# Wo and the broadcast reciprocal denominators loaded in whole-column pieces of 128 partitions, with one write of the reciprocals

## The chip, the cores and the metric

The kernel runs on one core of a Trainium2 chip. The metric is device time in microseconds (us). The core has a matrix engine (PE), a vector engine (DVE), an activation engine (ACT), GpSimd (POOL) and a sequencer without arithmetic (SP) that issues almost all DMAs of this kernel. One DMA is carried out by up to 16 DMA engines that the core has. On-chip memory is SBUF, 128 partitions of which each holds a row of every tile; matrix products land in PSUM, eight banks of 128 x 512 fp32.

## The reference

One transformer block over x of 2048 tokens by 1024, in bf16: an adaptive layer norm, linear attention with 32 heads of 32, a second adaptive layer norm, and a gated feed-forward part of width 3584.

```python
mod = (silu(c) @ w_mod).reshape(1, 6, 1, -1)
sa, ca, ga, sb, cb, gb = mod[:, 0], ..., mod[:, 5]

h = layernorm(x) * (1 + ca) + sa
q, k, v = heads(h @ wqkv)                    # 32 heads of 32
pq, pk = phi(q), phi(k)                      # phi(t) = (t + 1 if t > 0 else exp(t)) + 1e-6
kv = einsum('bhsd,bhse->bhde', pk, v)        # per head a 32 x 32 matrix
z  = einsum('bhsd->bhd', pk)
num = einsum('bhqd,bhde->bhqe', pq, kv)
den = einsum('bhqd,bhd->bhq', pq, z)[..., None] + 1e-6
x = x + ga * ((num / den).reshape(1, 2048, 1024) @ wo)

h = layernorm(x) * (1 + cb) + sb
x = x + gb * ((silu(h @ w_gate) * (h @ w_up)) @ w_down)
```

## The kernel before

**How it is written.** Operations are added in one program order to a small planner (`_Prog`, from line 120). Each engine carries out its own operations in that order. The planner derives from the SBUF intervals and PSUM banks that an operation touches which earlier operations of other engines it must wait for; partitions are not told apart. A DMA has a lane (a semaphore). An operation with `ninc=4` issues four DMAs on one lane, and a reader waits until all four have landed. Nearly all instructions are emitted through one helper, so in the profile they carry its line, 176, and are told apart by tile names.

**The stages.** From about 12 to 126 us: first layer norm, the q and k products, phi. From 126 to 186 us: sixteen groups `g_group(0..15)`, each of 16 matmuls, form G, the product of the normalized x and phi(k), for two halves of the heads (g 0 to 7 and g 8 to 15). From 186 to 220 us: the output projection `wo_part` with its residual. The rest, to 826 us: the feed-forward part in four chunks of 512 tokens.

**What lies in the stage of the change.** The loop `for g in range(16)` (from line 1038) sets the order on all engines:

- After group 0, `z_row` (line 962) writes the z row to DRAM and reads it back broadcast (`zb<-z_row`), and `wo_load(0)`, `wo_load(1)` (line 934) load Wo, 1 MB each, into the tile `wo` [128, 8, 1024]. Partition 32g+e and column block 4f+h of it hold row 512f + 128g + 32h + e of Wo.
- After group 1, `den()` (line 970) forms the denominators in PSUM bank 7 (partition 32ch + head, 512 tokens of chunk ch), adds 1e-6, takes the reciprocal and a bf16 copy `rcb`, writes it to the DRAM tensor `recip_den` [32, 2048], lets SP wait for that write, and loads it back broadcast over 32 partitions a head into `rb` [128, 8, 2048], 4 MB in eight DMAs. Both the write and the loads are issued on SP.
- At g 6 to 9, DVE scales Wo by ga, two column blocks each (`fold_ga`, line 1020).
- At g 7 to 14, DVE multiplies phi(q) by the reciprocals, one of eight head groups each (`scale_pq(g-7)`, line 992; in the profile `pqt<-pqt,rb`).
- DVE also empties the bank of each group (`g_evac`, line 953; `g<-ps,modcol,gtmp`), from g 6 on that of the group just before, and it does so ahead of that step's `fold_ga` and `scale_pq`.
- At g 10, `kvt_mm(0)` (line 995) needs G of groups 0 to 7; at g 11 and 12, `m_mm(0, ..)` (line 1005) multiplies its result by half of Wo into `mw`.
- At g 10, SP issues `stgx1`, 2 MB of w_mod into space that `rb` held, once `scale_pq(3)` is through.
- After group 15: SP reloads x into `xres`, in pieces; PE goes on with six matmuls of `wo_part`, then `kvt_mm(1)`, which needs G of groups 8 to 15, so `g_evac(15)`.

The DRAM view of Wo that the loads take is this (line 390), and `RDR` is `recip_den`:

```python
wov = A_wo.rearrange("(f g h e) n -> f g e h n", f=2, g=4, h=4)
```

Of the kernel before, what the change touches and what calls it, by code (L numbers as in the profile page):

```python
# [262 lines left out]
def bass_adaLN_cond__linear_attn_block__swiglu_ffn__prompt_kernel(  # L263
# [12 lines left out]
    S, D = A_x.shape[1], A_x.shape[2]  # L276
# [3 lines left out]
    NCH = 4  # L280
    NDT = D // 128
    NFT = F // 128
    NHG = D // 128
    EPS = 1e-5

    with ExitStack() as es:
# [6 lines left out]
        def T(name, off, shape, dt):  # L293
            n = 1
            for s_ in shape[1:]:
                n *= s_
            assert off % 32 == 0 and off + n * mybir.dt.size(dt) <= ARENA, (name, off, shape)
            return nc.alloc_sbuf_tensor_at(name, shape, dt, offset=base + off)
# [38 lines left out]
        RB = T("rb", 72 * KB, [128, NHG, S], BF16)  # L337
        WV = T("wv", 104 * KB, [128, NDT, D], BF16)
        HT = T("ht", 120 * KB, [128, 2, NDT, 512], BF16)
        WO = T("wo", 120 * KB, [128, NHG, D], BF16)  # L340
# [22 lines left out]
        RCB = T("rcb", 204 * KB, [128, 512], BF16)  # L363
# [18 lines left out]
        RDR = nc.dram_tensor("recip_den", [32, S], BF16).ap()  # L382
# [7 lines left out]
        wov = A_wo.rearrange("(f g h e) n -> f g e h n", f=2, g=4, h=4)  # L390
# [6 lines left out]
        P = _Prog()  # L397
# [534 lines left out]
        phi_flush()  # L932

        def wo_load(f):
            outs = [WO[32 * g:32 * g + 32, 4 * f:4 * f + 4, :] for g in range(4)]

            def fn(e, outs=outs, f=f):
                return [e.dma_start(out=o_, in_=wov[f, g]) for g, o_ in enumerate(outs)]

            P.add("sp", fn, reads=[], writes=outs, lane="wo%d" % f, ninc=4, tag="wo")  # L940

        G_BANKS = [0] + [next_bank() for _ in range(4)]

# [26 lines left out]
        def den():  # L970
            for hg in range(NHG):
                for ch in range(NCH):
                    P.pe("matmul", out=PS[32 * ch:32 * ch + 32, 7, :], lhsT=ZSEL[:, hg * 32:hg * 32 + 32],
                         rhs=PQT[:, hg, ch * 512:(ch + 1) * 512], start=(hg == 0), stop=(hg == NHG - 1),
                         skip_group_check=True)
            P.dve("tensor_scalar", out=DEN[:], in0=PS[:, 7, :], scalar1=1e-6, scalar2=None, op0=ALU.add)
            P.dve("reciprocal", out=RCP[:], in_=DEN[:])
            P.dve("tensor_copy", out=RCB[:], in_=RCP[:])
            wr = [P.dma("rdr%d" % ch, RDR[:, ch * 512:(ch + 1) * 512], RCB[32 * ch:32 * ch + 32, :])
                  for ch in range(NCH)]  # L980
            P.wait_for("sp", wr)
            for gh in range(2):
                outs = [RB[32 * hh:32 * hh + 32, 4 * gh:4 * gh + 4, :] for hh in range(4)]
                ins = [RDR.rearrange("(g x) s -> x g s", x=4)[hh, 4 * gh:4 * gh + 4].unsqueeze(0).to_broadcast([32, 4, S])
                       for hh in range(4)]

                def fn(e, outs=outs, ins=ins):
                    return [e.dma_start(out=o_, in_=i_) for o_, i_ in zip(outs, ins)]

                P.add("sp", fn, reads=[], writes=outs, lane="rb%d" % gh, ninc=4, tag="rb")  # L990

        def scale_pq(hg):
            P.dve("tensor_tensor", out=PQT[:, hg, :], in0=PQT[:, hg, :], in1=RB[:, hg, :], op=ALU.mult)
# [44 lines left out]
        for g in range(16):  # L1038
            g_group(g)
            while ev < g + 1 - (3 if g < 4 else 2 if g < 6 else 1):  # L1040
                g_evac(ev)
                ev += 1
            if g == 0:
                z_row()
                for f in range(2):
                    wo_load(f)
            if g == 1:
                mod_red()
                mod_fin_col(2, True)
                den()  # L1050
            if 6 <= g <= 9:
                fold_ga(2 * (g - 6))
                fold_ga(2 * (g - 6) + 1)
            if g == 10:
                kvt_mm(0)
            if 11 <= g < 13:
                m_mm(0, g - 11, [MB, 7, G_BANKS[4], 6])
            if 7 <= g < 15:
                scale_pq(g - 7)
            if g == 10:  # L1060
                P.dma("stgx1", STGX[0][:], wmv[:, :, 3072:4096])
# [51 lines left out]
        for st in range(NST):  # L1113
# [3 lines left out]
            if st < 4:  # L1117
                P.wait_for("sp", [done])
                if st < 3:
                    ch = st + 1  # L1120
# [127 lines left out]
```

## Time and profile before

| | us |
|---|---|
| median of 3 runs (lowest, highest) | 828.01 (827.72, 828.80) |
| the profiled execution | 827.71 |
| its span in the profile | 826.0 |
| PE busy | 816.3 |
| DVE busy | 312.2 |
| ACT busy | 197.0 |
| POOL busy | 41.0 |
| share of the time of 16 DMA engines taken by SP's queue | 53.8% |

Times inside the profile count from the start of the span; the execution's own time is 1.7 us more than the span. PE is busy for 99% of the span, and its granted clock is 1.00 in the stretch from 120 to 210 us. A matmul of 128 x 512 starts about 0.216 us after the one before it; the 379 ns that the profile gives for one include the time it takes to drain. "Landing" is the time from the issue of a DMA to its completion at its semaphore. "DMA share" is the mean busy share of the 16 DMA engines in a stretch of time; it can come out a little over 1.

### The profile page before, as it was taken

How to read it: one execution, taken by the hardware profiler on the slowest of the kernel's cores; microseconds unless marked ns; L12 is line 12 of the kernel's file. 1: busy time of each engine (PE TensorE's matmuls, PEld its weight loads, DVE VectorE, ACT ScalarE, POOL GpSimd, SP SyncE). 2: the span in 40 equal slices, each digit the busy share in tenths (PEclk: the TensorE clock that was granted, in tenths of full speed). 3: DMA queues.
4: the chain of work that ended last, by engine and by line, in shares of the span. 5: the costliest groups of instructions: out<-in, count | busy, mean ns of one | idle time of the engine just before them, and what ended most of it. 6: DMA issues, size and time to landing. Idle time of an engine off the chain costs nothing.

```text
span 826.0 us, 10436 instructions
## 1 busy us (share of the span) xinstructions
PE 816.3 (99%) x4243; PEld 375.9 (46%) x4322; DVE 312.2 (38%) x672; ACT 197.0 (24%) x338; POOL 41.0 (5%) x58
## 2 busy tenths in 40 slices
PE   8999999999999999999999999999999999999998
PEld 4544444444444444444444444444444444444444
DVE  5798988477945521111221112122111111221111
ACT  4758642123341111011111101111110111111011
POOL 1110000000130000020000003000000300000000
DMA  9969756865698995600455570045557004553000
GB/s 316 297 139 223 167 159 149 181 175 211 149 253 245 296 249 153 166 26 26 136 151 151 153 174 25 23 131 153 151 152 182 27 19 126 151 152 88 0 26 26
DMA packets 199392, 119.32 MB, mean 144 GB/s; under 512 B 58024, under 2 KB 183088, under 8 KB 199344
## 3 DMA queue, kind: packets, MB, share of 16 engines
q1 hardware_dynamic: 199328, 118.65, 53.8%
q8 instruction: 34, 0.56, 0.3%
q14 instruction: 14, 0.11, 0.0%
q10 hardware_dynamic: 16, 0.00, 0.0%
HBM read 100.67 MB, written 4.33 MB: 127 GB/s over the span
## 4 chain that ended last, share of the span: by engine, by line
PE 98%; issue 1%; DMA 0%; DVE 0%; POOL 0%; SPq 0%
PE ps L176 98%; DMA xres<-in_A_x_dram 0%; POOL rstd L176 0%; DVE xres L176 0%; DVE stats L176 0%; SPq L176 0%; DVE ht L176 0%; DVE ve L176 0%; DVE mv L176 0%; DVE modcol L176 0%
## 5 line engine op out<-in xcount | busy, mean ns | idle before, releaser
L176 PE MATMUL ps<-h2t,gug 128*128 128x512 bf16 x878 | 210.1, 379 | 0.9
L176 PE MATMUL ps<-h2t,guu 128*128 128x512 bf16 x878 | 209.9, 379 | 0.9
L176 DVE TENSOR_TENSOR at<-sg,ps 128x512 bf16<-128x512 bf16 x112 | 77.0, 687 | 282.8 <-PE ps L176 270.6
L176 ACT ACTIVATE sg<-ps 128x512 bf16<-128x512 f32 x112 | 66.9, 597 | 309.7 <-PE ps L176 298.3
L176 PEld LDWEIGHTS ps<-h2t,guu 128*128 128x128 bf16 x896 | 87.7, 98 | 105.7
L176 PEld LDWEIGHTS ps<-h2t,gug 128*128 128x128 bf16 x896 | 87.6, 98 | 105.5
L176 PE MATMUL ps<-wd_a,at 128*128 128x512 bf16 (+1 forms) x502 | 111.9, 377 | 0.5
L176 PE MATMUL ps<-ht,wqk 128*128 128x512 bf16 x499 | 110.7, 379 | 0.9 <-DVE ht L176 0.2
L176 PE MATMUL ps<-wd_b,at 128*128 128x512 bf16 (+1 forms) x377 | 84.6, 377 | 0.4
L176 PEld LDWEIGHTS ps<-wd_a,at 128*128 128x128 bf16 x512 | 50.1, 98 | 59.6
L176 DVE TENSOR_TENSOR ut<-att,gb_b 128x512 bf16<-128x512 bf16 (+1 forms) x32 | 13.6, 426 | 167.5 <-ACT att L176 167.5
L176 PEld LDWEIGHTS ps<-ht,wqk 128*128 128x128 bf16 x512 | 49.2, 98 | 58.9 <-DVE ht L176 1.0
L176 ACT ACTIVATE att<-ps 128x512 bf16<-128x512 f32 (+1 forms) x32 | 17.4, 591 | 182.1 <-PE ps L176 182.1
L176 PEld LDWEIGHTS ps<-wd_b,at 128*128 128x128 bf16 x384 | 37.6, 98 | 44.7
L176 PE MATMUL ps<-pk,xres 128*128 128x512 bf16 x250 | 55.4, 379 | 0.6 <-issue 0.5
L176 PE MATMUL ps<-mw,pqt 128*128 128x512 bf16 x249 | 55.4, 379 | 0.5 <-issue 0.2
L176 POOL TENSOR_SCALAR h2t<-h2t,modcol 128x512 bf16<-128x512 bf16 x32 | 26.5, 846 | 383.0 <-DMA h2t<-xn 383.0
L176 ACT ACTIVATE e<-ps 128x512 bf16<-128x512 f32 x56 | 33.3, 611 | 31.8 <-PE ps L176 15.8
L176 ACT ACTIVATE junk<-xres 128x1024 bf16<-128x1024 bf16 x26 | 27.6, 1063 | 45.9 <-DVE xres L176 34.2
L176 PEld LDWEIGHTS ps<-mw,pqt 128*128 128x128 bf16 x256 | 24.8, 98 | 30.0 <-issue 0.5
L176 PEld LDWEIGHTS ps<-pk,xres 128*128 128x128 bf16 x256 | 24.6, 98 | 30.1 <-issue 1.3
L176 DVE SCALAR_TENSOR_TENSOR xres<-ps,xres 128x512 bf16<-128x512 f32 x32 | 21.5, 688 | 11.6 <-PE ps L176 11.3
(111 smaller groups left out, 337.8 us busy)
## 6 DMA issues: line engine op xcount, KB each, us to landing
gug<-in_B_w_gate_dram SPq DMA_DIRECT2D x56, 512.0 KB, 4.0
guu<-in_B_w_up_dram SPq DMA_DIRECT2D x56, 512.0 KB, 5.3
xres<-in_A_x_dram SPq DMA_DIRECT2D x20, 256.0 KB, 4.4
rb<-recip_den SPq DMA_DIRECT2D x8, 512.0 KB, 11.7
stgx<-in_w_mod_dram SPq DMA_DIRECT2D x2, 2048.0 KB, 9.3
wd_a<-in_B_w_down_dram SPq DMA_DIRECT2D x4, 1024.0 KB, 7.7
out_dram<-xres SPq DMA_DIRECT2D x31, 128.0 KB, 1.7
xres<-in_A_x_dram SPq DMA_DIRECT2D x3, 1024.0 KB, 6.5
```

Source lines behind the costliest of these rows:

```text
L176: return getattr(e, method)(**kw)
```

## The change

All three transfers keep their bytes and their contents; their cut is another.

- Wo: four DMAs per half as before, but each brings one column block of all 128 partitions (128 rows of 2 KB), where before it brought four column blocks of 32 partitions (32 x 4 rows of 2 KB). On the DRAM side a piece is now a pattern of 4 x 32 rows: g steps by 128 rows, e by one.
- The reciprocals are written by one DMA from 128 partitions, where four wrote 32 partitions each. On the DRAM side the pattern is 4 chunks x 32 heads x 512 elements.
- The broadcast: eight DMAs as before, each now one head group hg for all 128 partitions: four rows of `recip_den`, each repeated 32 times (a step of 0). Before, each brought four head groups for 32 partitions. Each DMA has a lane of its own, so `scale_pq(hg)` waits for one DMA, where it waited for the four of its half.

```diff
         def wo_load(f):
-            outs = [WO[32 * g:32 * g + 32, 4 * f:4 * f + 4, :] for g in range(4)]
+            outs = [WO[:, 4 * f + h, :] for h in range(4)]
 
             def fn(e, outs=outs, f=f):
-                return [e.dma_start(out=o_, in_=wov[f, g]) for g, o_ in enumerate(outs)]
+                return [e.dma_start(out=o_, in_=wov[f, :, :, h, :]) for h, o_ in enumerate(outs)]
 
-            P.add("sp", fn, reads=[], writes=outs, lane="wo%d" % f, ninc=4, tag="wo")
+            P.add("sp", fn, reads=[], writes=[WO[:, 4 * f:4 * f + 4, :]], lane="wo%d" % f, ninc=4, tag="wo")
...
-            wr = [P.dma("rdr%d" % ch, RDR[:, ch * 512:(ch + 1) * 512], RCB[32 * ch:32 * ch + 32, :])
-                  for ch in range(NCH)]
-            P.wait_for("sp", wr)
-            for gh in range(2):
-                outs = [RB[32 * hh:32 * hh + 32, 4 * gh:4 * gh + 4, :] for hh in range(4)]
-                ins = [RDR.rearrange("(g x) s -> x g s", x=4)[hh, 4 * gh:4 * gh + 4].unsqueeze(0).to_broadcast([32, 4, S])
-                       for hh in range(4)]
+            wr = P.dma("rdr", RDR.rearrange("h (c s) -> c h s", c=NCH), RCB[:])
+            P.wait_for("sp", [wr])
+            for hg in range(NHG):
+                rb_ = RB[:, hg, :]
+                rows = RDR[4 * hg:4 * hg + 4, :].unsqueeze(1).to_broadcast([4, 32, S])
 
-                def fn(e, outs=outs, ins=ins):
-                    return [e.dma_start(out=o_, in_=i_) for o_, i_ in zip(outs, ins)]
+                def fn(e, rb_=rb_, rows=rows):
+                    return [e.dma_start(out=rb_, in_=rows)]
 
-                P.add("sp", fn, reads=[], writes=outs, lane="rb%d" % gh, ninc=4, tag="rb")
+                P.add("sp", fn, reads=[], writes=[RB[:, hg, :]], lane="rb%d" % hg, tag="rb")
```

## The prediction

> **What bounds the kernel now.** First the chain of work that ended last, on the page:
>
> ```profile
> PE 98%; issue 1%; DMA 0%; DVE 0%; POOL 0%; SPq 0%
> ```
>
> PE is the bound, so a transfer counts only where PE waits for it. I then asked for PE's waits from 125 to 205 us, the stretch that holds all changed transfers, and for DVE's:
>
> ```profile
> PE ps L176 <- issue: 0.6, 4, 0.2
> DVE pqt L176 <- DMA rb<-recip_den: 6.6, 1, 6.6
> ```
>
> The reader sees that PE loses 0.6 us there in four gaps, none to a DMA. DVE does wait 6.6 us for `rb`, but PE doesn't feel it. Thus nothing in this change can win more than 0.6 us; the question is what it can lose. The order of time of DVE, PE and SP shows how much room there is:
>
> ```profile
> 149.30 4.02 SPq L988 DMA_DIRECT2D rb<-recip_den  x8
> 161.28 1.22 DVE L176 TENSOR_TENSOR pqt<-pqt,rb 128x2048 bf16<-128x2048 bf16 x1 [6.65 <-DMA rb<-recip_den]
> 180.49 1.21 DVE L176 TENSOR_TENSOR pqt<-pqt,rb 128x2048 bf16<-128x2048 bf16 x1
> 186.07 0.75 DVE L176 SCALAR_TENSOR_TENSOR g<-ps,modcol,gtmp 128x512 bf16<-128x512 f32 x1 [2.70 <-PE ps L176]
> 187.26 1.19 PE L176 MATMUL ps<-g,wv 128*32 128x32 bf16 x128
> ```
>
> The first and last `scale_pq` start at 161.28 and 180.49; the last `g_evac` at 186.07, and `kvt_mm(1)`, which needs it, at 187.26. DVE works in order, so a late `rb` holds every `g_evac` behind it.
>
> Then the speed of the transfers, in stretches of 2 us (the last two columns are the share of 16 DMA engines and GB/s):
>
> ```profile
> 138.00:140.00 2.00, 2.00 (x11) 0.92 (x10) 2.00 (x1) 1.14 (x2) 0.00 (x0) 1.00 1.03 240
> 154.00:156.00 2.00, 2.00 (x11) 0.94 (x10) 0.63 (x2) 0.25 (x1) 0.00 (x0) 1.00 1.02 215
> 174.00:176.00 2.00, 1.84 (x24) 0.76 (x24) 1.10 (x3) 0.34 (x1) 0.00 (x0) 1.00 1.05 410
> 198.00:200.00 2.00, 2.00 (x11) 0.94 (x10) 1.40 (x3) 0.66 (x1) 0.00 (x0) 1.00 1.01 323
> ```
>
> In the first two, Wo and `rb` come 32 partitions at a time: 215 to 240 GB/s with all 16 engines busy, 13.4 to 15 each. In the others, w_mod and x come with 128 partitions: 323 to 410, 20 to 25.6 each. Over the four stretches from 196 to 204 the mean is 368, or 23 each.
>
> Last, how many engines a DMA uses:
>
> ```profile
> q1 hardware_dynamic: 199328, 118.65, 53.8%
> ...
> q10 hardware_dynamic: 16, 0.00, 0.0%
> ...
> cs<-in_c_dram ACTq DMA_DIRECT2D x1, 2.0 KB
> ```
>
> ACT's queue (q10) has one DMA, 8 rows of 256 B, and 16 packets: 8 rows and 8 more. SP's queue (q1) closes the same way: its plain DMAs move 141464 rows, its 28 transposes 53248 pieces of 256 B, and the 4616 packets left are 231 DMAs x 16, the three of 8 rows x 8 and the transposes x 32. So I read one closing packet per engine used: 16 where the pattern leads with 32 or 128 rows, 8 where it leads with 8.
>
> **The change, part by part.** Every changed DMA has 128 partitions on its SBUF side, but on its DRAM side its slowest step counts 4: g in Wo, the chunk in the write, the head in the broadcast. Before, both sides led with 32 (four leading DMAs of 32 rows each in the write). The 8-row DMAs show that the leading count limits the engines; if the smaller side decides, each changed DMA runs on 4 engines instead of 16. The rows do not show a DMA whose two sides differ, so this is the step on which all hangs. [...]
>
> The rate of four engines is bounded from the rows: 4 x 13.4 = 54 GB/s if they hinder each other as 16 did on 32 partitions, 4 x 25.6 = 102 if each runs as in the best stretch. I take 4 x 23 = 92, by the nearest row, the mean of loads that spread over 128 partitions, since the four write four different blocks of them.
>
> Step by step at 92 GB/s, times from the start of the span:
> - `zb`, issued at 133.94, is untouched and on 16 engines; data starts 1.6 us after an issue (`rb`: issued 149.30, moving from 150.9), and its 0.52 MB are through by about 137.3.
> - Wo, eight issues as before, 2.10 MB: 22.8 us, to 160.1 (before: 146.7). Its first half is there at about 149.4, so `fold_ga(0)` (149.90 before) hardly notices; the second half is read behind `rb`.
> - The write of the reciprocals, 0.13 MB behind Wo in the same queue: 1.4 us, to 161.5. Three issues of 0.42 us on SP go; SP waits anyway, so they are worth nothing. SP's wait ended 2.0 us after the data before (147.3 to 149.30): `rb` is issued at 163.5 instead of 149.30. Nothing else is queued on SP meanwhile but `stgx1`, which waits for `scale_pq(3)`, and POOL has no part.
> - `rb`, 4.19 MB, from 165.1: 45.6 us, 5.7 a DMA, to 210.7; DVE sees it 0.7 us later (160.6 to 161.28 before), 211.4. The finer lanes let `scale_pq(0)` start at about 171.5 rather than with the fourth DMA, which the later ones take back: the last one decides.
> - Behind it on DVE: `scale_pq(7)` and the last two `g_evac`, 1.13 + 0.67 + 0.75, and 0.4 to PE, 3.0 in all: `kvt_mm(1)` at 214.4 instead of 187.26, 27.1 us later. PE's earlier waits, for `g_evac(7)` at `kvt_mm(0)` and for the banks of `m_mm(0, ..)`, lie inside these 27.1, since all its work before `kvt_mm(1)` is then done.
> - After an idle stretch PE may start slow: its first eight matmuls of the span take 2.37 us where eight take 8 x 0.216 = 1.73, so +0.6 (between nothing and a few times that).
>
> What is late next: `stgx1` and the reload of x follow `rb` on the same queue. `scale_pq(3)` ends near 190, so their shares on the four busy engines come after 210.7: 2.1 MB / 16 / 23 GB/s = 5.7 us, and x's first tile 0.7 us: landed by about 217.8. Its reader started at 192.88 and moves to 220.0, so 2 us remain and I cost it at nothing; were the cover gone, a few us.
>
> Sum: 827.71 (profiled execution, 0.3 below the median 828.01) + 27.1 + 0.6 = **855.4 us**. The three transfers scale as 6.42 MB over the rate, 69.8 us of this path: at 102 GB/s 62.9, so 848.5; at 54 GB/s 119, so 904.5. The path breaks even with the old one at about 150 GB/s, that is from 6.5 engines on.
>
> **The rivals.** (1) Sixteen engines after all, because the SBUF side's 128 decides. Then Wo takes 2.10 MB / 368 = 5.7 us instead of 11, `rb` 11.4 instead of 19, the 6.6 us of DVE's wait go, and PE, which waits for none of it, gains between 0 and its 0.6: 827.1 to 828.0, the same. For it speaks that 128-partition loads reach 368 GB/s here; against it, that they all lead with 128 on both sides. It decides from 6.5 engines on. [...]
> (2) Four engines that get in each other's way. They walk through blocks of 32 partitions in step, and before, 16 engines on 32 partitions got 13.4 GB/s each. For it: that row. Against: the blocks differ. Time: 904.5.
> (3) The backlog behind `rb` holds x's reload past 220.0: 855.4 plus 2 to 5.
>
> **How the numbers follow.** Below 0.2% (1.7 us) a difference can't be told from none here. Four engines: 0.89, of which 0.65 between 20 and 50 us lost (the forecast with (3), 848 to 878), 0.14 beyond that up to (2), 0.10 at or just past the upper rate. Rival (1): 0.09, all of it within 0.2%. Something faster by over 1.7 us has no place in a PE that idles for 0.6: 0.02 for what I overlook. Slower 0.89, same 0.09, faster 0.02. The range takes in the bounds of the rate, 54 to 102 GB/s, with 4 us below for start times that overlap: 844 to 905, which leaves out rival (1) and little more.
>
> **What would show it.** SP's queue: twenty changed DMAs with 16 closing packets become seventeen with 4, 320 - 68 = 252 fewer: 199076 packets (199280 if they keep 16). DMA share near 0.25 and 90 GB/s while Wo and `rb` move; `rb` issued near 163, its last landing near 211; `scale_pq(0)` near 171; `kvt_mm(1)` near 214, with PE waits for DVE's `g` and `kvt` of about 27 us in all; all later stages as long as before. Wrong if the share stays near 1 at over 300 GB/s, if the four engines together pass 150 GB/s, or if their rate lies far from 92.

## The result and the profile after

The changed kernel takes 855.4 us (median of four runs, 854.02 to 856.27) against 828.2 (four runs of the kernel before): a ratio of 1.0329, 95% interval 1.0313 to 1.0345. The profiled execution took 855.38 us with a span of 853.6, 27.6 more than the span before.

The page of the changed kernel, its chain and the line of SP's queue:

```profile
PE 89%; DMA 7%; SPq 3%; issue 1%; DVE 0%; DVEq 0%
...
q1 hardware_dynamic: 199076, 118.65, 50.9%
```

The chain, 98% PE before, now runs through DMAs for 7% (4% `rb`, 2% the write of the reciprocals, 1% a load of the first 22 us that the change does not touch) and through SP for 3% (2% the issues of `rb`). The queue's packets fell by 252 from 199328, with the same bytes: the twenty changed DMAs that closed with 16 packets are now seventeen that close with 4.

Who PE waits for between 125 and 225 us (total, times, longest):

```profile
PE ps L176 <- DVE g L176: 17.8, 2, 13.6
PE ps L176 <- DVE kvt L176: 4.5, 1, 4.5
```

Before there was no such wait. PE's idle time in the whole span grew from 826.0 - 816.3 = 9.7 to 853.6 - 821.0 = 32.6, so by 22.9; its busy time grew by 4.7 with the same matmuls, some of which ran at half clock (below). Together these are the 27.6. The order of time of SP, DVE and PE shows what releases what:

```profile
134.86 11.73 SPq L938 DMA_DIRECT2D wo<-in_A_wo_dram  x8
146.63 4.41 SPq L176 DMA_DIRECT2D recip_den<-rcb  x1
160.71 25.62 SPq L986 DMA_DIRECT2D rb<-recip_den  x8
186.53 4.76 SPq L176 DMA_DIRECT2D stgx<-in_w_mod_dram  x1
```

```profile
169.61 1.23 DVE L176 TENSOR_TENSOR pqt<-pqt,rb 128x2048 bf16<-128x2048 bf16 x1 [14.31 <-DMA rb<-recip_den]
174.59 1.23 DVE L176 TENSOR_TENSOR pqt<-pqt,rb 128x2048 bf16<-128x2048 bf16 x1 [1.90 <-DMA rb<-recip_den]
...
189.56 1.23 DVE L176 TENSOR_TENSOR pqt<-pqt,rb 128x2048 bf16<-128x2048 bf16 x1 [1.90 <-DMA rb<-recip_den]
...
195.97 1.23 DVE L176 TENSOR_TENSOR pqt<-pqt,rb 128x2048 bf16<-128x2048 bf16 x1 [3.33 <-DMA rb<-recip_den]
...
203.71 1.23 DVE L176 TENSOR_TENSOR pqt<-pqt,rb 128x2048 bf16<-128x2048 bf16 x1 [5.86 <-DMA rb<-recip_den]
...
210.30 1.22 DVE L176 TENSOR_TENSOR pqt<-pqt,rb 128x2048 bf16<-128x2048 bf16 x1 [4.70 <-DMA rb<-recip_den]
```

```profile
212.25 1.04 PE L176 MATMUL ps<-mw,pqt 128*128 128x512 bf16 x2 [13.64 <-DVE g L176]
213.50 1.49 PE L176 MATMUL ps<-mw,pqt 128*128 128x512 bf16 x3 [0.22 <-issue]
214.92 1.22 PE L176 MATMUL ps<-g,wv 128*32 128x32 bf16 x128
```

Every scale of phi(q) waits for its own piece of `rb`. The first five start 5.0 us apart, the last three gaps are 6.4, 7.7 and 6.6. `kvt_mm(1)` starts at 214.92, 27.7 us later than before, and everything after it keeps that distance: the first residual on DVE starts at 220.56, before at 192.88.

The stretches of 2 us of the changed kernel (the last three columns are the granted clock of PE, the share of 16 DMA engines and GB/s):

```profile
152.00:154.00 2.00, 2.00 (x11) 0.88 (x9) 0.65 (x1) 0.00 (x0) 0.00 (x0) 1.00 0.26 102
...
162.00:164.00 2.00, 2.00 (x11) 0.94 (x10) 0.00 (x0) 0.00 (x0) 0.00 (x0) 1.00 0.25 66
164.00:166.00 2.00, 2.00 (x11) 0.92 (x10) 0.00 (x0) 0.00 (x0) 0.00 (x0) 1.00 0.27 74
...
176.00:178.00 2.00, 1.22 (x6) 0.37 (x4) 1.68 (x3) 0.72 (x1) 0.00 (x0) 1.00 0.26 106
...
196.00:198.00 2.00, 2.00 (x11) 0.88 (x9) 1.86 (x2) 0.05 (x1) 0.00 (x0) 1.00 1.05 229
...
202.00:204.00 2.00, 0.00 (x0) 0.00 (x0) 0.29 (x1) 0.00 (x0) 0.00 (x0) 0.50 0.26 104
```

While Wo (at 153) and `rb` (at 177) move alone, a quarter of the engines is busy, at 25.5 to 26.5 GB/s each. `rb` begins slower (66 and 74). At 196 the followers are under way too, and all engines are busy. PE ran dry at 198.6; its clock is 1.00 until 202 and 0.50 from there to 215.6: it fell 3.4 us after PE ran dry. In the two waits before it, from 167.4 and from 177.2, it fell to 0.50 after 3.8 and 4.3 us, and was back at 1.00 by 174.8 and 185.0.

### The profile page after: what moved, and what is told of

Its sections match the earlier page's. It is cut to its first block, busy times and chain, and to the rows that moved or that the text cites. A ratio compares the mean times of both kernels' runs of the same rounds, so it can differ in the third digit from the quotient of the medians.

```text
span 853.6 us, 10432 instructions
## 1 busy us (share of the span) xinstructions
PE 821.0 (96%) x4243; PEld 376.9 (44%) x4322; DVE 313.6 (37%) x672; ACT 197.1 (23%) x338; POOL 40.8 (5%) x58
## 3 DMA queue, kind: packets, MB, share of 16 engines
q1 hardware_dynamic: 199076, 118.65, 50.9%
## 4 chain that ended last, share of the span: by engine, by line
PE 89%; DMA 7%; SPq 3%; issue 1%; DVE 0%; DVEq 0%
PE ps L176 89%; DMA rb<-recip_den 4%; SPq L986 2%; DMA recip_den<-rcb 2%; DMA wsa<-in_w_mod_dram 1%; SPq L176 1%; DVE g L176 0%; DVE ht L176 0%; DVE xres L176 0%; DVE modcol L176 0%; DVE pqt L176 0%; DVEq L247 0%
## 5 line engine op out<-in xcount | busy, mean ns | idle before, releaser
L176 PE MATMUL ps<-pk,xres 128*128 128x512 bf16 x250 | 57.5, 389 | 0.8 <-issue 0.7
L176 POOL TENSOR_SCALAR h2t<-h2t,modcol 128x512 bf16<-128x512 bf16 x32 | 26.3, 838 | 383.0 <-DMA h2t<-xn 383.0
L176 ACT ACTIVATE junk<-xres 128x1024 bf16<-128x1024 bf16 x26 | 27.6, 1063 | 47.1 <-DVE xres L176 34.2
```

Of the source, the lines that this page charges most:

```text
L176: return getattr(e, method)(**kw)
```

## The experiments

The theory: a DMA runs on as many engines as the smaller of the leading counts of its two sides allows, here 4, and the end of the last `rb` piece sets the loss. The rivals: only the broadcast is slow, because it reads rows again and again; SP, held while it issues, is the cause; the small write is.

**Each part alone.** Three kernels take one part of the change each: the `wo_load` hunk; the `den` hunk (write and broadcast); and of that only the write.

```diff
# Wo alone: of the change, only
-            outs = [WO[32 * g:32 * g + 32, 4 * f:4 * f + 4, :] for g in range(4)]
+            outs = [WO[:, 4 * f + h, :] for h in range(4)]
...
# write and broadcast alone: of the change, the next edit and this one (RB by head groups)
-            for gh in range(2):
-                outs = [RB[32 * hh:32 * hh + 32, 4 * gh:4 * gh + 4, :] for hh in range(4)]
+            for hg in range(NHG):
+                rows = RDR[4 * hg:4 * hg + 4, :].unsqueeze(1).to_broadcast([4, 32, S])
...
# the write alone: of the change, only
-            wr = [P.dma("rdr%d" % ch, RDR[:, ch * 512:(ch + 1) * 512], RCB[32 * ch:32 * ch + 32, :])
-                  for ch in range(NCH)]
-            P.wait_for("sp", wr)
+            wr = P.dma("rdr", RDR.rearrange("h (c s) -> c h s", c=NCH), RCB[:])
+            P.wait_for("sp", [wr])
```

Wo alone:

> Only the Wo loads are changed; the write and the broadcast stay as before. Theory (a DMA runs on as many engines as the smaller leading count, here 4, at 25.5 GB/s each): Wo moves at 102 GB/s until about 159 us, the write lands behind it, rb is issued near 160.5 and moves at 215 GB/s on 16 engines, so its halves are there near 172.5 and 182; kvt_mm(1) about 10 us late, 838 us (835 to 841). Rival (only the broadcast is slow, because it reads a row of DRAM 32 times): Wo at over 300 GB/s, no loss, 828.

Measured: 838.6 us, ratio 1.0125 (1.011 to 1.014), 10.4 us lost. SP's queue has 199232 packets, 96 fewer than before, 12 for each of the eight pieces of Wo. `rb` was issued at 160.44, as late as in the change (160.71), where these pieces move at 102 GB/s with a share of 0.26, and scaled first at 172.34. These bytes are read once, so this part of the loss does not come from rereading rows.

Write and broadcast alone:

> Wo as before; the write and the broadcast of the reciprocals as in the change. Theory: rb issued near 150.5, its first piece there 8.9 us later, the others 5.0 us apart, and the last three held up by 5.7 us by the loads that follow, as in the changed kernel; kvt_mm(1) about 17 us late, 845 us (842 to 848). Rival (the loss sits in Wo, or in SP that is held while it issues Wo): 828 to 832.

Measured: 843.14 us, ratio 1.0181 (1.0165 to 1.0196), 15.0 us lost. `rb` was issued at 148.12, the pieces came 5.0 us apart, the last three 6.6, 7.5 and 6.8. The first came 8.4 us after the issue and the issue was 2.4 us earlier than I had put it, hence 2 us less than my middle. The two parts add up to 25.4 of the 27.2 us.

The write alone:

> Only the write of the reciprocals is changed: one DMA for four. Theory: 0.13 MB on 4 engines takes 1.3 us instead of 0.6, rb is issued about 1 us later, and DVE has 1.8 us to spare before PE would wait: 828.0 (827.4 to 828.8). Rival (the write to DRAM with 4 KB steps is the slow piece): 830 or more.

Measured: 828.37 us, ratio 1.0001 (0.9991 to 1.0011). `rb` was issued at 148.85, no later than before: the write is worth nothing.

**The leading count, with the 128 partitions kept.** The reciprocals are written twice or four times, so that the DRAM side of each broadcast leads with 8 or 16 rows. Wo is loaded as before.

```diff
-        RDR = nc.dram_tensor("recip_den", [32, S], BF16).ap()
+        RDR = nc.dram_tensor("recip_den", [64, S], BF16).ap()            # 128 rows for 16
...
# the broadcast, from that of the change
-                rows = RDR[4 * hg:4 * hg + 4, :].unsqueeze(1).to_broadcast([4, 32, S])
+                rows = RDR[8 * hg:8 * hg + 8, :].unsqueeze(1).to_broadcast([8, 16, S])
```

> Wo as before. The reciprocals are written twice into a scratch tensor of 64 rows, so that each of the eight broadcast loads (128 partitions, one head group, own lane) has 8 rows repeated 16 times on its DRAM side. Theory: 8 engines, 204 GB/s, the last piece near 173, before DVE needs it: 828.0 (827.4 to 828.8), though the DMAs are of 128 partitions as in the change; SP's queue 199392 packets (128 rows more, 8 x 8 closing packets fewer). Rival (repeated reads or 128-partition writes from a row of 4 KB are slow by themselves): rb near 100 GB/s again and 843 or more; 199456 packets if it is not the leading count that sets the engines.

> As the one with 8 rows, with four copies of the reciprocals, so that each broadcast load has 16 rows repeated 8 times. Theory: 16 engines, over 300 GB/s, 4.2 MB in 12 to 14 us; DVE's wait of 6.6 us before its first scale goes, PE had not waited for it: 828.0 (827.2 to 828.5); 199712 packets. Rival (repeated reads are slow): near 100 to 215 GB/s.

Sixteen rows: 828.07 us, ratio 1.0002 (0.9992 to 1.0011); eight rows: 838.97, ratio 1.0132 (1.0115 to 1.0149), a miss. The lines of SP's queue and a stretch while `rb` moves, first for 8 rows, then for 16:

```profile
q1 hardware_dynamic: 199392, 118.78, 53.9%
...
160.00:162.00 2.00, 2.00 (x11) 0.94 (x10) 1.23 (x2) 0.00 (x0) 0.00 (x0) 1.00 0.52 127
```

```profile
q1 hardware_dynamic: 199712, 119.04, 53.6%
...
160.00:162.00 2.00, 2.00 (x11) 0.93 (x10) 2.00 (x4) 0.72 (x1) 0.00 (x0) 1.00 1.03 240
```

The packets are those forecast to the last one, and the shares are a half and the whole: the leading count does set the engines. With 16, DVE's first scale starts at 154.68 without a wait, PE waits for nothing but issue, and the time is that of before. But the engines do not bring 25.5 GB/s each: 8 bring 127 together, 16 bring 240, where 204 and over 300 were expected.

**What holds 8 and 16 engines back.** Five more kernels measure the rate by itself, with other rows in the broadcast's place.

```diff
# from the kernel with 16 rows, to different rows in 16 blocks of 8 (8 blocks of 16: j=17, 136 rows and 0:16)
-                rows = RDR[16 * hg:16 * hg + 16, :].unsqueeze(1).to_broadcast([16, 8, S])
+                rows = B_w_gate[100 * hg:100 * hg + 144, 0:S].rearrange("(i j) s -> i j s", j=9)[:, 0:8, :]
# or to one row for all 128 partitions
+                rows = RDR[4 * hg:4 * hg + 1, :].to_broadcast([128, S])
# from the kernel with 8 rows, to 8 rows of w_gate, 108 rows apart
-                rows = RDR[8 * hg:8 * hg + 8, :].unsqueeze(1).to_broadcast([8, 16, S])
+                rows = B_w_gate[17 * hg:17 * hg + 864, 0:S].rearrange("(i j) s -> i j s", j=108)[:, 0:1, :].to_broadcast([8, 16, S])
# or to scratch rows that start 7168 B apart
+        RDR = nc.dram_tensor("recip_den", [64, 3584], BF16).ap()[:, 0:S]
```

> A measurement of the rate by itself. As the kernel with 16 repeated rows, but each broadcast load brings 128 different rows of w_gate, 16 blocks of 8 neighbouring rows, in place of the reciprocals (phi(q) is scaled by the wrong numbers; the division is left out). Theory A (blocks: the engines walk through blocks of partitions in step and meet at the same ones of SBUF's entries, whatever is read): rb at about 240 GB/s, as with 16 repeated rows. Theory B (reading a row of DRAM again and again is what is slow): over 330 GB/s, as for other loads of 128 different rows.

> The other half of that measurement: each broadcast load repeats one row of the reciprocals over all 128 partitions, so that the leading count is 128 on both sides (all heads of a group are divided by the first one's denominator; the other three are left out). Theory A (blocks): over 330 GB/s, since both sides lead with 128 as in the loads of x. Theory B (repeated reads): 240 GB/s or less.

> 128 different rows of w_gate in 8 blocks of 16 neighbouring rows, in place of the reciprocals (the division is left out). Theory A (blocks): 8 engines at about 127 GB/s together, as with 8 repeated rows, and about 839 us again. Theory B (repeated reads): 8 x 25.5 = 204 GB/s, and 828 us.

> As the kernel with 8 rows repeated 16 times, but the rows are rows of w_gate that lie 108 rows apart (the division is left out). If the repetition is what holds 8 engines at 127 GB/s, rb moves at about 127 GB/s again and the time is near 839. If it was where the rows lie (eight neighbouring rows of a scratch tensor of 256 KB), rb moves at 170 to 210 GB/s as with different rows of w_gate, and the time is 828.

> The kernel with 8 rows repeated 16 times again, but a row of the scratch tensor starts 7168 B after the one before it, as in w_gate, instead of 4096 B. If the step of 4096 B held the 8 engines at 127 GB/s, rb moves at 170 GB/s or more and the time is 828.0 (827.4 to 828.8). If it is something else about a scratch tensor that was just written, 127 GB/s and 839 us.

One stretch each while `rb` moves: 16 blocks of different rows, one row for all, 8 blocks of different rows, 8 repeated rows of w_gate, 8 repeated scratch rows 7168 B apart.

```profile
160.00:162.00 2.00, 2.00 (x11) 0.91 (x10) 2.00 (x4) 0.72 (x1) 0.00 (x0) 1.00 1.02 248
```

```profile
156.00:158.00 2.00, 2.00 (x11) 0.94 (x10) 1.83 (x3) 0.72 (x1) 0.00 (x0) 1.00 0.94 328
```

```profile
160.00:162.00 2.00, 2.00 (x11) 0.91 (x10) 2.00 (x4) 0.72 (x1) 0.00 (x0) 1.00 0.51 205
```

```profile
160.00:162.00 2.00, 2.00 (x11) 0.89 (x10) 2.00 (x4) 0.00 (x0) 0.00 (x0) 1.00 0.50 160
```

```profile
160.00:162.00 2.00, 2.00 (x11) 0.88 (x9) 2.00 (x3) 0.34 (x1) 0.00 (x0) 1.00 0.54 166
```

With 16 engines it makes no difference whether rows repeat (240 against 248), and a load that leads with 128 on both sides is faster even when all read one row (258 to 330 in its six stretches from 152 to 164, though not over the 330 expected). So a lead of 16, not rereading, goes with some 245 GB/s; that the engines then meet at the same partitions is argued and not shown. With 8 engines neither theory holds. Different rows start at 168 and climb to 211 within 14 us, so 8 engines can pass 200; repeated rows of w_gate run at 160 to 213 from 154 us on; repeated scratch rows 4096 B apart stay at 121 to 137, and 7168 B apart they run at 133 to 174. So the step of 4096 B, with which the size of the scratch tensor changes too, costs 8 engines some 30 GB/s of 158; how, and what the rest of the gap to 200 is, stays open.

The times tell where the loss begins. At 158 GB/s (the kernel with 7168 B) the median is 828.47, ratio 1.0025 (0.9999 to 1.0051), but three of its ten runs took 834 to 836, which fits a kernel on the edge (the profiled run is one of 827.94). Of the others, one run each, 16 blocks took 827.79, 8 blocks 827.98, 8 rows of w_gate 828.56 and one row for all 827.72 us. At 127 GB/s the loss is 11 us, and the rate is only part of it: the scales of that kernel start 4.2 us apart at first, and the last three gaps, with w_mod and x under way, are 6.0, 6.1 and 5.7. At 4.2 the last would have started near 186 instead of 191.43, an estimate from these gaps; so 5 of the 8.8 us by which its `kvt_mm(1)` is late (196.05 against 187.26) would be due to the loads that follow.

**The loads that follow.**

```diff
-                scale_pq(g - 7)
-            if g == 10:
-                P.dma("stgx1", STGX[0][:], wmv[:, :, 3072:4096])
+                scaled = scale_pq(g - 7)             # scale_pq now returns its operation
         g_evac(15)
+        P.wait_for("sp", [scaled])
         for st in range(4):
             P.dma("xr%d" % st, XRES[:, st, :], xv[:, st, :])
+        P.dma("stgx1", STGX[0][:], wmv[:, :, 3072:4096])
```

> The changed kernel, but SP issues the first reload of x and then the 2 MB of w_mod only after the last scale_pq, where the changed kernel issues w_mod after the fourth and x after group 15. Theory (these loads, which share the 16 engines, held up the last three pieces of rb by 5.7 us): rb's eight pieces 5.0 us apart to the end, kvt_mm(1) 5.7 us earlier, 849.7 us (848 to 851.5). Rival (the last pieces are slow for another reason, such as SP being held while it issues them): 855 or, since the followers then come late, more.

Measured: 850.38 us, ratio 1.0267 (1.0252 to 1.0282) to before, 5.0 less than the change. Its last scales and its `kvt_mm(1)`:

```profile
188.65 1.23 DVE L176 TENSOR_TENSOR pqt<-pqt,rb 128x2048 bf16<-128x2048 bf16 x1 [1.90 <-DMA rb<-recip_den]
193.65 1.23 DVE L176 TENSOR_TENSOR pqt<-pqt,rb 128x2048 bf16<-128x2048 bf16 x1 [1.92 <-DMA rb<-recip_den]
198.64 1.22 DVE L176 TENSOR_TENSOR pqt<-pqt,rb 128x2048 bf16<-128x2048 bf16 x1 [3.10 <-DMA rb<-recip_den]
203.62 1.23 DVE L176 TENSOR_TENSOR pqt<-pqt,rb 128x2048 bf16<-128x2048 bf16 x1 [3.09 <-DMA rb<-recip_den]
```

```profile
208.23 1.24 PE L176 MATMUL ps<-g,wv 128*32 128x32 bf16 x128
```

The pieces now come 5.0 us apart to the last. SP was held here for as long (24.5 us over the eight issues, 25.6 in the change), so it is the followers that slowed the last three. Nor did SP set the pace before that: in the change the share stays at 0.25 to 0.30 in every stretch from 162 to 192, so the four engines did not run out of issued work. Of the 6.7 us that `kvt_mm(1)` gained (214.92 to 208.23), 1.6 were given back behind it, 0.8 of them in one gap of PE.

How the followers slow `rb` is not shown. That `rb` had to queue behind them on its four engines does not fit the changed kernel's trace: when `rb` is through, a quarter of the engines stays busy until 217, at 101 GB/s:

```profile
212.00:214.00 2.00, 1.53 (x4) 0.66 (x6) 0.85 (x2) 0.00 (x0) 0.00 (x0) 0.50 0.26 101
214.00:216.00 2.00, 2.00 (x131) 1.17 (x129) 0.00 (x0) 0.00 (x0) 0.00 (x0) 0.59 0.26 101
```

From 211 to 217 that is 0.6 MB, more than a quarter of the 2.1 MB of w_mod, so these engines seem to have taken up the followers' shares only then. But while both move, from 192 to 201, all 16 engines together bring 226 GB/s, where w_mod alone brought up to 410.

## Why the prediction was right

The way was right, and the mechanism: four engines, a late last piece of `rb`, and PE waiting behind it. That the time came out at 855.4 to the tenth is luck, since three terms were off and cancelled. By the prediction's own steps:

- **Four engines.** Right: 199076 packets, share 0.26. The step on which all hung, an assumption in the prediction, is shown by the runs with 4, 8 and 16 leading rows, at 128 partitions each (shares 0.26, 0.52 and 1.03). The number of different rows does not set it: Wo's pieces hold 128 of them and ran at a share of 0.26, and one row for all 128 partitions ran at 0.80 to 1.08. What other pairs of counts would give, no run tells.
- **92 GB/s.** Too low: 102 for Wo, 105 for `rb` (0.524 MB in 4.99 us), 25.5 to 26.3 an engine. The nearest row was the mean of loads on 16 engines; four alone run like the best stretch of those, 25.6. So `rb` was issued at 160.71 instead of 163.5, and the first scale started at 169.61 instead of about 171.5, though `rb` began at 66 GB/s. Seven pieces of 5.0 instead of 5.7 us would have brought the last scale to 204.5, 5 us sooner yet.
- **"What is late next."** Half of it was right. `rb` does hold up the followers: w_mod, issued at 186.53, landed 28.7 us later (9.0 to 9.6 before), and a quarter of the engines was busy until 217, where I had x's first tile by 217.8. It cost nothing, as I had put it: the first reader of x at 220.56 and that of w_mod at 223.45 wait for no DMA. What I left out is the reverse: the followers hold up `rb`, for 5.7 us. The engines that `rb` left idle took up w_mod and x at once (share 0.28 from 190 to 192 and 0.98 from 192 to 194; the issue of w_mod ended at 191.29), and the three last pieces pay. With it the last scale starts at 210.30; the prediction had 211.4.
- **From the last scale to `kvt_mm(1)`.** 4.6 us instead of 3.0. I had all of PE's work before `kvt_mm(1)` done by then; in fact the six matmuls of `wo_part` wait for a bank that a late `g_evac` empties (PE at 212.25 waits for DVE's `g`), and they run at half clock (0.50).
- **A cold start of PE, 0.6.** It is not behind `kvt_mm(1)`, where I put it: this runs 1.37 us to the next matmul, 1.36 before. It lies ahead of it, in the 4.6. Its source was misread as well: the eight matmuls are not the first of the span, five more of their shape run ahead of them, from 2.61 on, at a granted clock of 1.00; the 2.37 us run to the end that the profile gives for the last, and to the start of the next group it is 2.26, so 0.5. The waits of PE that I put at about 27 us came as 22.3 of waiting and 4.7 of slower matmuls.
- **The rest.** The write and its three issues: nothing, as forecast. Wo's first half was there for `fold_ga(0)`, 150.56 against 149.90. The stretches after 220 are as long as before.

The sum against the forecast of 214.4 for `kvt_mm(1)`: -1.9 for the first piece, -5.0 for the seven others, +5.7 for the followers, +1.6 for the tail, hence 214.8; measured 214.92.

Of the rivals, sixteen engines after all fell with the packet count. Four engines in each other's way (54 GB/s) fell too, though low rates turned up: `rb` starts at 66, and 8 engines stay at 127. In what order engines walk through the partitions no run shows. "From 6.5 engines on" was wrong as put: what decides is the rate and not the count. The prediction's sum put the limit at about 150 GB/s; with Wo as before it lies between 128 (11 us lost) and 158 (on the edge), and eight engines were above it in three kernels and below it in one.

## What to carry to other kernels

Look at both sides of a DMA: a load that fills 128 partitions from a pattern whose slowest step counts 4 ran on 4 engines here, at 102 GB/s, where four loads of 32 partitions each ran on 16, at 203 to 240. The packets of the queue told the engines: each plain DMA here closed with one packet per engine that it used (252 fewer in the change). And when a transfer becomes the end of a chain, ask which later transfers the queue lets in beside it; here they cost it 5.7 of the 40.7 us between the first scale and the last.

## What the runs showed of the hardware that was not expected

- SP was held by the DMAs on four engines: the eight issues of Wo took 11.73 us instead of 4.40 for the same bytes, and one issue of `rb` 10.17 us against 0.43 before. It cost nothing that shows, since the four engines stayed busy (share 0.25 to 0.30 from 162 to 192).
- 128 partitions and 16 engines do not make a fast load by themselves: 236 to 254 GB/s when the DRAM side leads with 16 (154 to 166 us), 258 to 330 when both sides lead with 128 and all read one row, 391 to 411 for w_mod, which leads with 128 on both sides and reads different rows (172 to 176 us of the same kernels). Before, 16 engines on 32 partitions ran at 203 to 240. What sets these rates apart, no run shows.
- With 8 engines and repeated rows, a step of 7168 B instead of 4096 B between the scratch rows raised the rate from about 128 to 158 GB/s (means from 152 to 170 us) and the median time fell from 838.97 to 828.47 us.
